# A fused attention and gated-FFN kernel: half batch 1's decay is added by matmuls of its own, and the first values are loaded ahead of its keys

## The chip, the cores and the metric

The kernel runs on one core of one Trainium2 chip. A core has TensorE (matmul), VectorE, ScalarE, GpSimd (POOL in the profile) and SyncE (SP, which here only issues DMAs)[...]. The time is device microseconds; the number to compare is the median of several runs. The profile is of one single execution, with a time and a span of its own.

## The reference

Forgetting attention over 8 batches of 8 heads, 576 positions and 64 elements a head, followed by an FFN with a convolution as a gate:

```python
scores = (1/8) * (q @ k.T)                    # per head, 576 x 576
cum    = cumsum(log(clip(f, 1e-4, 1)))        # per head
scores = where(causal, -1e9, scores + cum[:, None] - cum[None, :])
x      = softmax(scores) @ v                  # heads side by side: 576 x 512
h      = relu(x @ w_in)                       # 576 x 1024
c      = 3-tap convolution of h over the positions, per column
out    = (h * sigmoid(c)) @ w_out             # 576 x 512
```

The difference of the two cum terms is called the decay.

## The kernel before

**Tiling.** The work goes by half batches of four heads (hb, 0 to 15); a pair i is two heads of one of them. For each half batch, q and k are brought in by transposing DMAs that read each float32 as two 16-bit halves (`load_qk`, L110). One tile `stq` of 128 partitions and one tile `stk` hold them, four tiles of each in a ring. Odd partitions hold the high halves, which are bfloat16 numbers; the even ones hold the low halves, which have to be made zero. That is `clamp` (L119), an integer multiply and add on VectorE. The free even partitions carry the decay: partitions 96 and 98 of `stk` get the high and low part of the cumulated logs, with ones opposite in `stq`; partition 126 of `stq` gets the high part, with minus one opposite. So one matmul gives the score with its decay (`scores`, L298).

For half batch 0 these rows come from a quick computation of their own (`rows_first`, L122, issued from ScalarE's and POOL's queues). For half batch 1 and later the clamp covers only partitions 0 to 95 and the others are written by DMA on POOL's queue: the constants by `fill` (L132) from a tile `consts`, which `fill_sources` (L544 to L546) sets on VectorE, and the decay rows by `rows_of`, from SBUF for half batch 1 (L140 to L142) and from a copy `kd` in DRAM for the others (L144, L146). These DMAs wait for the transposes, because they write into the same tile.

**Steps of a pair.** `tail_scores` (L304, once a half batch), `diag_scores` (L330 adds the causal mask by a matmul) and `off_scores` write PSUM; ScalarE takes exponentials (L310, L338, L324); `pv` (L356) multiplies with the values; `norm` (L367, L369) divides on VectorE. Values arrive by plain DMAs in float32 (`load_v`, L163, five instructions for a half batch) in one of two buffers `vf` and are cast on VectorE (L170 to L173). The values of batch b go to buffer b mod 2. A batch's output is transposed on TensorE (L393, L401) and copied out of PSUM (L411, L413).

**FFN.** For each batch eight units of 128 columns: `moe1` (L425, eight matmuls), Relu on ScalarE (L438), two convolution steps on VectorE (L455, L457), tanh on ScalarE (L467), the gate on VectorE (L475). The Relu's output has four buffers `ht`, so the fifth unit's Relu waits for the first unit's gate. `moe2` (L487) multiplies with w_out. The w_in load is released by the first norm (L151, L634). The four w_out loads on POOL's queue (L155) are each released by a one-element memset on VectorE (`hold`, L151).

**Order.** The beginning, to L269, is written out by hand. All after it are tasks, each with engine costs in us, a due time (`key`), dependencies and buffers. At build time `play` walks through an estimated time and gives each engine, when it is free, the ready task with the smallest key. The order that comes out is fixed: on the chip each engine runs its queue in that order, and an instruction whose operand is late holds what is behind it. `lag` is the time that `play` adds for an arrival; SP's loads follow an estimate of the DMA stream (`dma`, `dma_free`, `QUEUED`). After L269 comes first half batch 0 and 1's attention; batch 0's FFN then runs beside half batches 2 and 3, and so on. SP's queue at the start is: q and k of half batch 0 in four pieces (L189, L190), q and k of half batch 1 (L235), the values of both half batches (L251, L252), then the planned loads: q, k, then values of each half batch.

Of the kernel before, what the change touches and what calls it, by code (L numbers as in the profile page):

```python
# [9 lines left out]
FP32 = mybir.dt.float32  # L10
FP16 = mybir.dt.float16
BF16 = mybir.dt.bfloat16
# [6 lines left out]
def kernel(  # L19
# [102 lines left out]
    def rows_first(p, eng):  # L122

        tq, tk, c, r = stq_t[0], stk_t[0], slice(2 * p * S, 2 * (p + 1) * S), slice(64 * p, 64 * (p + 1))
        eng.dma_start(tq[126:127, c], khi4[r, :])
        eng.dma_start(tk[96:97, c], khi4[r, :])
        eng.dma_start(tk[98:99, c], klo4[r, :])
# [7 lines left out]
    def rows_of(hb):  # L135

        tq, tk = stq_t[hb % RING], stk_t[hb % RING]
        c = slice(hb * HH, (hb + 1) * HH)
        if hb == 1:
            nc.gpsimd.dma_start(tk[96:97, 0:HS], khi_sb[c, :])  # L140
            nc.gpsimd.dma_start(tk[98:99, 0:HS], klo_sb[c, :])
            nc.gpsimd.dma_start(tq[126:127, 0:HS], khi_sb[c, :])  # L142
            return
        nc.gpsimd.dma_start(tq[126:127, 0:HS], kd[0:1, c, :].rearrange("j h s -> j (h s)"))  # L144
        row = HS + 64
        nc.gpsimd.dma_start(bass.AP(tensor=tk.tensor, offset=int(tk.offset) + 96 * row, ap=[[2 * row, 2], [1, HS]]),  # L146
                            kd[:, c, :].rearrange("j h s -> j (h s)"))

    def hold(w):

        nc.vector.memset(w[0:1, 0, 0:1], 0.0)  # L151
# [83 lines left out]
    load_qk(1, 0, 4)  # L235
    for side in range(2):
        clamp(0, side, 0, 2)
    rows_first(0, nc.scalar)

# [10 lines left out]
    nc.vector.memset(vf_t[0][0:1, 0, 0, 0:1], 0.0)  # L250
    load_v(0, 0, HH)  # L251
    load_v(0, HH, H)  # L252
# [14 lines left out]
    for t in range(NHT):  # L267
        nc.gpsimd.memset(ht_t[t][:, :, 0:HT_0], 0.0)
        nc.gpsimd.memset(ht_t[t][:, :, HT_0 + S:HT_W], 0.0)  # L269

# [25 lines left out]
    def scores(sc, hb, k0, q0, w, start=True, stop=True):  # L296

        nc.tensor.matmul(sc, stk_t[hb % RING][:, k0:k0 + 128], stq_t[hb % RING][:, q0:q0 + w],  # L298
                         start=start, stop=stop, skip_group_check=True)
# [242 lines left out]
    def fill_sources():  # L542
        z = consts.bitcast(FP32)
        nc.vector.memset(z, 0.0)  # L544
        nc.vector.memset(z[0:2, :], PAIR)
        nc.vector.memset(z[32:33, :], MINUS)  # L546

    CLAMPS, HALVES, LANDING = 8, 16, 3.0
    HELD, POOLED = 4, 4
    WAITS = ((3, 0), (3, 1), (4, 0), (4, 1))  # L550
# [8 lines left out]
    t_fsrc = task({"DVE": 3.1}, [], -9, fill_sources)  # L559
    for hb in range(NHB):  # L560
        key = 2 * hb - 5.5
        ring = [x for j in range(2) for x in t_qk[hb - RING, j]] if hb >= RING else []
        b = hb // 2
        even, landed = [], []
        for s in range(2):
            if hb == 1:
                x = task({"ACT": 0.01}, [], -9, lambda: None, lag=(0.3, 3.8)[s])
            elif hb:
                last = x = task({"SP": 3.0}, ring, key + 0.1 * s, lambda hb=hb, s=s: load_qk(hb, 0, 4, s),
                                lag=LANDING, dma=3.1, behind=last)  # L570
            if hb:
                landed.append(x)
            if hb:
                t = (stq_t, stk_t)[s][hb % RING]
                rows = [(100, 14, 19)] if s else [(96, 15, 0)] + [(0, 48, 33)] * (hb >= CLAMPS)
                even.append(task({"POOL": 0.55 * len(rows)}, [t_fsrc, x], 2 * hb - 3.5,
                                 lambda t=t, rows=rows: [fill(t, *x) for x in rows],
                                 lag=LANDING + 1.0, dma=0.3 if s or hb < CLAMPS else 1.2))
            if hb and (s or hb < CLAMPS):
                even.append(task({"DVE": 0.9}, [x], (2 * hb - 3 if hb > 1 else -5) + 0.2 * s,  # L580
                                 lambda hb=hb, s=s: clamp(hb, s, 0, 4, 96)))
        t_half = None
        if b == 0 and hb < 2:
            t_half = task({"ACT": 0.01}, [], -9, lambda: None, lag=(6.5, 9.3)[hb])
            t_v[b] = t_half
        elif hb < HALVES:
            last = t_half = task({"SP": 3.2}, [t_cast[hb - 4, p] for p in range(2)] if b >= 2 else [], key + 0.2,
                                 lambda b=b, h=HH * (hb % 2): load_v(b, h, h + HH), lag=2.3, dma=3.0, behind=last)
        elif hb % 2 == 0:
            last = t_v[b] = task({"SP": 3.5}, [t_cast[2 * b - j, p] for j in (4, 3) for p in range(2)] if b >= 2 else [],  # L590
                                 key + 1.2, lambda b=b: load_v(b), lag=2.3, dma=6.0, behind=last)
# [4 lines left out]
        if hb:  # L596
            t_rows[hb] = even + [task({"POOL": 1.1 if hb > 1 else 1.6}, landed, 2 * hb - 3.6 if hb > 1 else -9 if hb > 1 else -1.0,
                                      lambda hb=hb: rows_of(hb), lag=LANDING + 1.0)]
        else:
            t_rows[hb] = []  # L600
        for p in range(2):
            t_cast[hb, p] = task({"DVE": 0.75 if p == 0 else 0.42},
                                 [t_half or t_v[b]] + ([t_pv[2 * hb - 5, 1]] if hb >= 3 else []), 2 * hb - 1.1 + 0.5 * p,
                                 lambda hb=hb, p=p: cast_v(hb, p, nc.vector), lag=0.2)

        for p in range(2):
# [10 lines left out]
            x = task({"PE": 0.9}, t_rows[hb], i + 0.1, lambda i=i: diag_scores(i), take="sc")  # L617
            t_qk[hb, p] = [t_tail, x]
            mask = task({"ACT": 1.02}, [x], i + 0.1, lambda i=i: diag_exp(i), take="pm", give=[("sc", x)])
            for s in range(2):  # L620
                x = task({"PE": 0.46}, t_rows[hb], i + 0.2 + 0.4 * s, lambda i=i, s=s: off_scores(i, s),
                         take="sc")
                t_qk[hb, p].append(x)
                exps[s] = task({"ACT": 1.02}, [x] + ([t_pv[i - 2, s]] if i >= 2 else []), i + 0.2 + 0.4 * s,
                               lambda i=i, s=s: off_exp(i, s), give=[("sc", x)])
# [5 lines left out]
            t_norm[i] = task({"DVE": 1.05}, [t_pv[i, 1]], i - 0.0, lambda i=i: norm(i) if i else [norm(i), hold(w_in_f16)],  # L631
                             take="xn" if i % PPB == 0 else None, give=[("O", t_pv[i, 0])])
            if i == 0:
                t_win = task({"POOL": 1.0}, [t_norm[0]], -0.5, lambda: nc.gpsimd.dma_start(  # L634
                    w_in_f16, moe_w_in.rearrange("(cc p) ff -> p cc ff", p=128)), lag=2.0, dma=6.5)
        if hb % 2:
# [10 lines left out]
    start = [PPB * (b0 + nb) + 1.0 for b0, nb in GROUPS]  # L647
    start += [start[-1] + 4.0, start[-1] + 6.0]
    t_exp, t_late = [], []
    for g, (b0, nb) in enumerate(GROUPS):  # L650
# [3 lines left out]
        for ff in range(NFF):  # L654
            key = start[g] + 0.8 * (start[g + 1] - start[g]) * ff / NFF
            relus = []
            for t in range(nt):
# [5 lines left out]
                relus.append(task({"ACT": 0.18 + w / 1200.0}, [x] + relus[0:1], key + 0.05 * t - 1.5,  # L663
# [10 lines left out]
            t_gate[g, ff] = task({"DVE": 0.1 + n / 1800.0 if g == LAST else 0.2 + n / 1050.0}, [x], key - 1.5, lambda g=g, ff=ff: gate(g, ff),  # L674
# [36 lines left out]
    AHEAD, QUEUED = 3.0, 8.0  # L711

    def play():
        busy = {"PE": 11.5, "ACT": 12.0, "DVE": 12.0, "POOL": 14.0, "SP": 19.0}
        ready = {e: [] for e in busy}
        dma_free, clock = 21.5, 0.0
# [112 lines left out]
```

## Time and profile before

| what | us |
| --- | --- |
| median of 7 runs | 272.42 (271.61 to 273.86) |
| profiled execution, its own time | 270.95 |
| its span, first to last instruction | 269.0 |
| TensorE, VectorE, ScalarE busy | 240.9, 226.6, 212.1 |
| first exponential (L338) | 12.22 |
| first score matmul of half batch 1, 2, 3, 4 | 23.88, 41.47, 55.42, 63.96 |
| first FFN matmul (L425) | 36.89 |
| first convolution step (L455) | 39.54 |

The page of the profile gives busy time by engine and, as rows of digits, by 40 slices of 6.7 us each; PEclk is the TensorE clock that was granted, in tenths. Other views give busy time by stretch, the chain of work that ended last (start, duration, what), and the instructions in order of time; there "xN" joins N instructions, and in square brackets is how long the engine was idle before and what it waited for. "SPq", "POOLq" or DMA_DIRECT2D on POOL are issues of DMAs.

### The profile page before, as it was taken

What the parts mean: (1) busy time and instruction counts of PE and PEld (TensorE: products, weight loads), DVE (VectorE), ACT (ScalarE), POOL (GpSimd) and SP (SyncE); (2) the same over time, 40 slices, a digit from 0 to 9 for tenths busy, and PEclk for the clock granted to TensorE, in tenths of its full rate; (3) what the DMA queues carried; (4) which work ended last, traced back from release to release, by engine and by line L of the source; (5) the groups of instructions that cost most, each with busy time, mean ns of one, the idle gap of its engine ahead of it and who ended that gap; (6) DMA issues with size and microseconds to landing.
All of it is one profiled execution on the core that took longest, in us unless ns stands there. A gap on an engine that the chain in (4) does not pass through costs nothing.

```text
span 269.0 us, 6621 instructions
## 1 busy us (share of the span) xinstructions
PE 240.9 (90%) x2602; PEld 165.2 (61%) x2602; DVE 226.6 (84%) x401; ACT 212.1 (79%) x347; POOL 59.4 (22%) x124
## 2 busy tenths in 40 slices
PE   2876769877999999999999999999999999989990
PEld 1344537655767677676777677667776767555640
DVE  5965449999799999999989989999899999978751
ACT  5163639899879999989988999989899998577552
POOL 4481110641222140432404040404110100000000
PEclk9979979999999999999999999999999999999997
DMA  7999999999999999999999999999410202022015
GB/s 143 218 201 198 222 195 227 168 229 178 198 215 196 239 247 168 232 254 264 226 167 226 186 270 162 186 130 257 113 58 23 80 0 77 5 117 80 0 49 225
DMA packets 121284, 44.58 MB, mean 166 GB/s; under 512 B 115560, under 2 KB 116596, under 8 KB 121254
## 3 DMA queue, kind: packets, MB, share of 16 engines
q1 hardware_dynamic: 115088, 32.00, 68.8%
q0 software_dynamic: 5840, 12.01, 17.0%
q8 instruction: 20, 0.33, 0.6%
q10 hardware_dynamic: 326, 0.17, 0.3%
q14 instruction: 10, 0.08, 0.1%
HBM read 13.99 MB, written 9.58 MB: 88 GB/s over the span
## 4 chain that ended last, share of the span: by engine, by line
PE 62%; DMA 9%; DVE 7%; SPq 6%; issue 6%; ACT 6%; POOL 0%; ACTq 0%; DVEq 0%; POOLq 0%
PE mm L425 18%; PE mm L487 18%; PE sc L298 10%; PE O L356 7%; DMA stk<-in_k_dram 6%; SPq L110 4%; PE sc L330 4%; DMA vf<-in_v_dram 2%; PE sc L500 2%; SPq L163 2%; DVE u L457 2%; DVE u L455 2%; PE mm L393 2%; ACT ht L438 1%; DMA out_dram<-ob 1%
## 5 line engine op out<-in xcount | busy, mean ns | idle before, releaser
L425 PE MATMUL mm<-xt,w_in_f 128*128 128x288 f16 x512 | 79.7, 289 | 1.7 <-DVE xt L413 0.4
L298 PE MATMUL sc<-stq,stk 128*128 128x128 bf16 (+3 forms) x576 | 67.4, 243 | 5.6 <-ACT pm L338 3.2
L324 ACT ACTIVATE po<-sc 128x1024 f16<-128x1024 f32 x64 | 64.6, 1028 | 2.1 <-PE sc L298 1.7
L438 ACT ACTIVATE ht<-mm 128x288 f16<-128x288 f32 x128 | 52.0, 414 | 11.5 <-PE mm L425 10.3
L487 PE MATMUL mm<-w_out_f,hg 128*128 128x512 f16 x248 | 58.4, 379 | 0.7 <-ACT xt L411 0.6
L425 PEld LDWEIGHTS <-w_in_f 128*128 128x128 f16 x512 | 47.7, 99 | 18.5 <-issue 3.2
L298 PEld LDWEIGHTS <-stk 128*128 128x128 bf16 x576 | 42.5, 99 | 26.9 <-issue 7.8
L455 DVE SCALAR_TENSOR_TENSOR u<-ht,cwt 128x576 f32<-128x576 f16 x64 | 51.6, 812 | 5.4 <-ACT ht L438 4.7
L457 DVE SCALAR_TENSOR_TENSOR u<-ht,cwt,u 128x576 f32<-128x576 f16 x64 | 51.5, 812 | 0.5
L475 DVE SCALAR_TENSOR_TENSOR hg<-hg,ht 128x576 f16<-128x576 f16 x56 | 41.7, 752 | 3.7 <-ACT hg L467 3.3
L467 ACT ACTIVATE hg<-u,cwt 128x576 f16<-128x576 f32 x56 | 43.4, 780 | 1.0 <-DVE u L457 0.9
L338 ACT ACTIVATE pm<-sc 128x1024 f16<-128x1024 f32 x32 | 32.9, 1027 | 11.8 <-PE sc L298 11.6
L487 PEld LDWEIGHTS <-hg 128*128 128x128 f16 x248 | 23.6, 98 | 24.2 <-issue 0.9
L356 PE MATMUL O<-va,po 128*128 128x65 f16 x640 | 36.5, 194 | 1.2 <-ACT po L324 1.0
L356 PE MATMUL O<-va,pm 128*128 128x65 f16 x256 | 31.1, 194 | 3.0 <-DVE xn L369 1.8
L356 PEld LDWEIGHTS <-po 128*128 128x128 f16 x640 | 30.5, 97 | 2.4 <-ACT po L324 1.8
L132 POOL DMA_DIRECT2D stq<-consts x23 | 12.2, 533 | 73.0 <-PE sc L298 26.2
L356 PEld LDWEIGHTS <-pm 128*128 128x128 f16 x256 | 24.3, 98 | 5.7 <-DVE xn L369 2.7
L369 DVE TENSOR_TENSOR xn<-O,rc 128x640 f16<-128x640 f32 x32 | 26.4, 825 | 1.1
L330 PE MATMUL sc<-trib,identb 128*128 128x512 bf16 x64 | 24.5, 383 | 1.5 <-ACT po L324 1.4
L511 ACT ACTIVATE ob<-mm 128x512 f32<-128x512 f32 x23 | 13.7, 598 | 11.0 <-PE mm L487 10.7
L522 POOL DMA_DIRECT2D out_dram<-ob x10 | 7.5, 748 | 39.9 <-ACT ob L511 20.8
(112 smaller groups left out, 223.2 us busy)
## 6 DMA issues: line engine op xcount, KB each, us to landing
vf<-in_v_dram SPq DMA_DIRECT2D x64, 128.0 KB, 3.9
out_dram<-ob POOLq DMA_DIRECT2D x10, 512.0 KB, 5.1
out_dram<-ob SPq DMA_DIRECT2D x10, 256.0 KB, 2.1
stq<-consts POOLq DMA_DIRECT2D x8, 216.0 KB, 4.5
vf<-in_v_dram SPq DMA_DIRECT2D x16, 64.0 KB, 5.2
w_in_f<-in_moe_w_in_dram POOLq DMA_DIRECT2D x1, 1024.0 KB, 9.1
w_out_f<-in_moe_w_out_dram POOLq DMA_DIRECT2D x4, 256.0 KB, 5.9
out_dram<-ob SPq DMA_DIRECT2D x2, 512.0 KB, 2.8
```

Source lines behind the costliest of these rows:

```text
L298: nc.tensor.matmul(sc, stk_t[hb % RING][:, k0:k0 + 128], stq_t[hb % RING][:, q0:q0 + w], start=start, stop=stop, skip_group_check=True)
L324: nc.scalar.activation(p_of[i, s][:, 0:1024], sc_of.pop((i, s)), AF.Exp, scale=SCALE)
L330: nc.tensor.matmul(sc[:, 512 * s:512 * (s + 1)], identb, trib, start=True, stop=False, skip_group_check=True)
L338: nc.scalar.activation(p_of[i, 2], sc_of.pop((i, 2)), AF.Exp, scale=SCALE)
L356: nc.tensor.matmul(O[:, s, 65 * Q:65 * (Q + 1)], w, va[:, h, m, :], start=(m == 0), stop=(m == Q))
L425: nc.tensor.matmul(ps[:, 0:w], w_in_f16[:, cc, 128 * ff:128 * (ff + 1)], xt[:, cc, w * t:w * (t + 1)], start=(cc == 0), stop=(cc == NCC - 1))
L438: nc.scalar.activation(ht[:, 0, HT_0 + w * t:HT_0 + w * (t + 1)], ps[:, 0:w], AF.Relu)
L455: nc.vector.scalar_tensor_tensor(u, hl, cwt[:, ff, 0:1], hc, op0=ALU.mult, op1=ALU.add)
L457: nc.vector.scalar_tensor_tensor(u, hr, cwt[:, ff, 1:2], u, op0=ALU.mult, op1=ALU.add)
L467: nc.scalar.activation(hv, u, AF.Tanh, scale=cwt[:, ff, 2:3])
L475: nc.vector.scalar_tensor_tensor(hv, hv, 1.0, hc, op0=ALU.add, op1=ALU.mult)
L487: nc.tensor.matmul(ps, chunk(g, ff, c), w_out_f16[:, ff, :], start=(ff == 0), stop=(ff == NFF - 1))
```

## The change

It has four parts.

1. Half batch 1's decay is no longer in `stq` and `stk`. Two new tiles, `dk` and `dq`, lie in the second values buffer, which is free until batch 1's values come. `decay_tiles` sets them on ScalarE: `dk` to zero with minus one in partitions 0 to 2, `dq` to one. `load_decay` writes three rows, on POOL's queue right behind half batch 0's: the high part and the low part into `dk`, the high part into `dq`. Each score matmul of half batch 1 is followed by one of the same shape with these tiles, over all 128 partitions, into the same PSUM. Its clamp covers all 128 partitions, and its two constant fills and three rows are gone. Batch 1's values wait until half batch 1's scores are done.
2. On SP half batch 0's values go ahead of half batch 1's q and k, which are issued later in the program; the values of half batch 1 follow. The memset that held the first values is gone.
3. The constants for half batches 2 and later are set by three tasks on VectorE behind norm(1), no longer at the start. Two w_out loads are released by a later task of half batch 3.
4. Costs, lags and due times of the planner change, with the order that follows from them: norm earlier against clamps and casts, gate later, Relu earlier; half batches 6 and 7 have their q cleared by a DMA fill and no longer by the clamp (`CLAMPS`); from half batch 8 on, values come in whole batches (`HALVES`). Five tasks `warm` of two matmuls each, of which nothing is used, get the lowest priority behind the last pv of half batch 0.

In the resulting order TensorE runs the first pv ahead of off_scores of pair 1; conv_weights after the first off_scores of pair 3; the warm tasks between half batch 1's last pieces; and ten moe1 tiles ahead of half batch 2's scores, where there were six. On VectorE norm(2) and norm(3) are ahead of the clamp of half batch 2's keys, and that clamp comes behind the first convolution step. On ScalarE half batch 2's first exponentials come behind the Relu of the fifth FFN unit and three tanh.

```diff
         c = slice(hb * HH, (hb + 1) * HH)
-        if hb == 1:
-            nc.gpsimd.dma_start(tk[96:97, 0:HS], khi_sb[c, :])
-            nc.gpsimd.dma_start(tk[98:99, 0:HS], klo_sb[c, :])
-            nc.gpsimd.dma_start(tq[126:127, 0:HS], khi_sb[c, :])
-            return
...
+    def decay_tiles(hb, dk, dq):
+        dec_of[hb] = dk, dq
+        for t, x in ((dk, 0.0), (dk[0:3], MINUS), (dq, PAIR)):
+            z = t.bitcast(FP32)
+            nc.scalar.activation(z, one1[0:z.shape[0]].broadcast_to(z.shape), AF.Copy, bias=x, scale=0.0)
+
+    def load_decay(hb):
+        (dk, dq), c = dec_of[hb], slice(HH * hb, HH * (hb + 1))
+        nc.gpsimd.dma_start(dk[0:1, 0:HS], khi_sb[c, :])
+        nc.gpsimd.dma_start(dk[1:2, 0:HS], klo_sb[c, :])
+        nc.gpsimd.dma_start(dq[2:3, 0:HS], khi_sb[c, :])
...
-    load_qk(1, 0, 4)
     for side in range(2):
         clamp(0, side, 0, 2)
     rows_first(0, nc.scalar)
+    load_v(0, 0, HH)
+    load_qk(1, 0, 4)
+    load_v(0, HH, H)
+    early = vf_t[1].rearrange("p h k d -> p (h k d)")
+    decay_tiles(1, early[:, 0:HS // 2 + 32].bitcast(BF16), early[:, HS // 2 + 32:HS + 32].bitcast(BF16))
...
     rows_first(1, nc.gpsimd)
-    nc.vector.memset(vf_t[0][0:1, 0, 0, 0:1], 0.0)
-    load_v(0, 0, HH)
-    load_v(0, HH, H)
+    load_decay(1)
     nc.gpsimd.dma_start(kd[0], khi_sb)
...
+    def warm():
+        ps = mm_pool.tile([128, 512], FP32, name="mm")
+        for t in range(2):
+            nc.tensor.matmul(ps, identb, trib, start=True, stop=True)
...
-                         start=start, stop=stop, skip_group_check=True)
+                         start=start, stop=stop and hb not in dec_of, skip_group_check=True)
+        if hb in dec_of:
+            dk, dq = dec_of[hb]
+            nc.tensor.matmul(sc, dk[:, k0:k0 + 128], dq[:, q0:q0 + w],
+                             start=False, stop=stop, skip_group_check=True)
...
-    CLAMPS, HALVES, LANDING = 8, 16, 3.0
+    CLAMPS, HALVES, LANDING = 6, 8, 3.0
-    WAITS = ((3, 0), (3, 1), (4, 0), (4, 1))
+    WAITS = ((3, 1), (3, 1), (4, 0), (4, 1))
+    WARM = {0: 5}
...
-    t_fsrc = task({"DVE": 3.1}, [], -9, fill_sources)
+    t_dec = {1: task({"ACT": 0.01}, [], -99, lambda: None, lag=4.5)}
     for hb in range(NHB):
+        if hb == 2:
+            t_fsrc = None
+            for z in ((0, 96, 0.0), (0, 2, PAIR), (32, 33, MINUS)):
+                t_fsrc = task({"DVE": 1.03}, [t_norm[1], t_fsrc], 3.0, lambda z=z: fill_source(*z))
...
-            if hb:
+            if hb > 1:
                 t = (stq_t, stk_t)[s][hb % RING]
...
-                even.append(task({"DVE": 0.9}, [x], (2 * hb - 3 if hb > 1 else -5) + 0.2 * s,
-                                 lambda hb=hb, s=s: clamp(hb, s, 0, 4, 96)))
+                even.append(task({"DVE": 0.9}, [x], (2 * hb - 2 if hb > 1 else -5) + 0.2 * s,
+                                 lambda hb=hb, s=s: clamp(hb, s, 0, 4, 96 if hb > 1 else 128)))
...
-            t_norm[i] = task({"DVE": 1.05}, [t_pv[i, 1]], i - 0.0, lambda i=i: norm(i) if i else [norm(i), hold(w_in_f16)],
+            t_norm[i] = task({"DVE": 1.05}, [t_pv[i, 1]], i - 0.5, lambda i=i: norm(i) if i else [norm(i), hold(w_in_f16)],
...
+        if hb in WARM:
+            x = None
+            for _ in range(WARM[hb]):
+                x = task({"PE": 0.44}, [t_pv[2 * hb + 1, 1], x], 999, warm, take="mm", lag=0.05)
+                gives = tasks[x][4]
+                gives.append(("mm", x))
...
-                relus.append(task({"ACT": 0.18 + w / 1200.0}, [x] + relus[0:1], key + 0.05 * t - 1.5,
+                relus.append(task({"ACT": 0.18 + w / 1200.0}, [x] + relus[0:1], key + 0.05 * t - 2.0,
...
-            t_gate[g, ff] = task({"DVE": 0.1 + n / 1800.0 if g == LAST else 0.2 + n / 1050.0}, [x], key - 1.5, lambda g=g, ff=ff: gate(g, ff),
+            t_gate[g, ff] = task({"DVE": 0.1 + n / 1800.0 if g == LAST else 0.2 + n / 1050.0}, [x], key - 0.0, lambda g=g, ff=ff: gate(g, ff),
```

## The prediction

> **What bounds the kernel now.** I read the busy rows by slice first, then busy time by stage, then the chain that ended last over the first 42 us, then the order of instructions there. The page:
>
> ```profile
> span 269.0 us, 6621 instructions
> ...
> PE   2876769877999999999999999999999999989990
> ...
> DVE  5965449999799999999989989999899999978751
> ...
> PEclk9979979999999999999999999999999999999997
> ```
>
> From slice 10 on TensorE is full, and before that it is not. Stages say how much is missing (columns: stretch, length, PE, PEld, DVE, ACT, POOL busy, clock, DMA share, GB/s):
>
> ```profile
> 12.00:19.00 7.00, 4.60 (x34) 2.62 (x32) 4.91 (x8) 4.81 (x6) 6.51 (x27) 0.79 1.05 202
> 19.00:24.00 5.00, 2.85 (x70) 2.48 (x68) 1.54 (x5) 1.39 (x2) 1.68 (x3) 0.96 1.22 187
> 24.00:33.00 9.00, 7.21 (x117) 5.41 (x116) 5.39 (x17) 6.20 (x7) 1.01 (x2) 1.00 1.17 226
> 33.00:37.00 4.00, 1.11 (x18) 0.80 (x15) 2.12 (x4) 0.68 (x1) 1.01 (x2) 0.94 1.26 158
> 37.00:42.00 5.00, 5.00 (x32) 3.18 (x31) 2.35 (x5) 2.72 (x8) 0.50 (x1) 0.71 1.14 240
> 42.00:50.00 8.00, 7.66 (x104) 5.90 (x103) 7.79 (x15) 8.00 (x14) 2.72 (x4) 1.00 1.15 165
> 50.00:60.00 10.00, 7.21 (x83) 5.03 (x81) 9.88 (x22) 8.46 (x16) 4.91 (x7) 1.00 1.28 240
> 60.00:80.00 20.00, 17.99 (x251) 13.49 (x248) 17.86 (x30) 16.99 (x27) 4.52 (x8) 1.00 1.22 196
> 80.00:100.00 20.00, 19.91 (x234) 14.22 (x233) 18.89 (x31) 18.27 (x31) 6.07 (x11) 1.00 1.08 227
> ```
>
> TensorE idles 2.4+2.15+1.8+2.9 us between 12 and 37, 0.3 us to 50, 2.8 us to 60 and 2.0 us to 80; from 80 to 235 all its gaps add to 1.0 us. So the start-up is bound by what arrives when, 42 to 68 by VectorE and ScalarE, the rest by TensorE. A microsecond won before 68 is kept to the end; one won later is not. The chain and the order of work show the start-up's links (start, us, what):
>
> ```profile
> 23.23 10.71 DMA stk<-in_k_dram
> 33.94 0.03 issue
> 33.96 0.88 DVE stk L119
> 34.84 0.14 DVE rc L367
> ...
> 36.89 4.76 PE mm L425 x24
> ```
>
> ```profile
> 19.39 0.50 POOL L142 DMA_DIRECT2D stq<-khi_sb  x1
> ...
> 23.88 0.28 PE L298 MATMUL sc<-stq,stk 128*128 128x64 bf16 x4 [0.98 <-DMA stq<-khi_sb]
> ...
> 42.91 1.02 ACT L338 ACTIVATE pm<-sc 128x1024 f16<-128x1024 f32 x1
> ...
> 47.10 0.73 POOL L155 DMA_DIRECT2D w_out_f<-in_moe_w_out_dram  x1 [5.82 <-DVE w_out_f L151]
> ...
> 55.42 0.27 PE L304 MATMUL sc<-trit,identb 128*128 128x256 bf16 x1
> ```
>
> Half batch 1's scores wait until 23.88 for a decay row issued at 19.39. The normalisation of its last heads (L367, L369) stands on VectorE behind the clamp of half batch 2's keys, which land at 33.94; so the first FFN matmuls start at 36.89. And POOL is held 5.82 us by a w_out load, so half batch 3's decay rows go out only at 47.83 to 49.4 and its scores start at 55.42.
>
> **The change part by part**
>
> *Half batch 1 starts earlier: -2.0 us.* Its three decay rows now go into two ready tiles in the values buffer, straight after half batch 0's rows (POOL, 12.33): issued to 13.9, and at the 4.0 to 4.8 us that these rows took before, landed by 18.7. Its keys go to SP behind five value loads. Those took 3.2 us of SP (12.62 to 15.78), so the keys land at 15.76+3.2 = 19.0 and are clamped by 21.7. What is then last is half batch 0. Its exponentials end at about 21.2, not 20.57, because the first PV matmuls, whose values come early, now stand ahead of the next scores while the clock is at half; the last PV takes 0.45. First scores: 21.9 for 23.88.
>
> The fills of those tiles are three ScalarE instructions of 1152 to 1184 elements; 1024 elements took 1.02, so 3.4 us. ScalarE is free from 8.4, when its row DMAs are out, to the first exponential at 12.22: nothing. If they overran, each microsecond would be one on half batch 0. On POOL the two constant fills and three rows at 17.09 to 19.89 go away and three issues (1.6 us) come in ahead of the kd stores and the memsets; these are needed at 28.6 (kd) and about 17 (the memset that ended at 13.9, now 15.6): nothing. The three constant memsets (3.1 us of VectorE) move to about 23 to 28, where VectorE has gaps (5.39 busy of 9 from 24 to 33): nothing. The w_in load keeps its trigger, norm(0). One wait is new: batch 1's first values, issued by SP at 30.88, overwrite these tiles and so wait for half batch 1's last scores. Behind them on SP are half batch 3's queries and keys. The last scores should end at 21.9+8.9 = 30.8: nothing; each microsecond more delays those keys by one, and they have some 4 us to spare (landed near 45, rows issued at 48.4).
>
> *Its scores cost double: +2.9 us.* 36 added matmuls stream 16x256 + 16x128 + 4x64 = 6400 columns. A 512-column trib matmul is followed by the next after 0.22 us (23.99, 24.21), so they take 2.7 us; each of five warm tasks (two 512-column matmuls) takes 0.43. From first scores to the end of norm(2) the old order took 31.97-23.88 = 8.1 us and was paced by ScalarE. The new one is paced by TensorE: tail 0.33, diagonal twice 1.33, off-diagonal four times 0.87, transpose 0.45, PV twice 0.45, conv weights 0.6, warm twice 0.43 make 9.3. norm(2) no longer hides: conv_weights is behind the third off-diagonal, at +7.55, and its eight small VectorE operations (1.4), the query clamp (0.87) and the norm (1.05) follow it: +10.95.
>
> *norm(3) ahead of the key clamp: -1.35 us.* From norm(2) to the first FFN matmul took 36.89-31.97 = 4.9. Now PV 0.5, warm 0.43, PV 0.45, waits 0.15, norm 1.05 and the old 1.0 for transposes and copies: 3.55. FFN start: 21.9+10.95+3.55 = 36.4, so -0.5.
>
> *The clock: -1.05 us.* The 24 matmuls at 36.89 took 4.76, or 198 ns each; later groups of eight take 0.98, or 122 ns. The granted clock is 0.50 from 36.5 to 39.5. The first convolution came 2.65 after the first matmul; at full clock two groups, two Relus of 0.41 and the hand-over make 1.6. Does the clock hold? It dropped at 16.0 and 36.5, when TensorE had been busy some 1.4 and 0.9 us of the 3.4 before, and held at 22.8 and 26.2 with some 2.2. The Trainium skill, "TensorE: Matmul & The Clock Gate", Part 1 (What's actually happening), gives a free-running window of about 3.4 us and half rate after an idle one. By that rule neither drop had to come, and none could after the change, where no window is idle: -1.05 for certain. By the row a partly busy window drops too. With the new order TensorE is busy about 2.7 us of the last 3.4, or 1.75 if the window falls worse, which is between the drops and the holds; then the term is +0.15. I go by the row and take the clock as held.
>
> *The convolution stretch: +0.3 us.* The first convolution starts at 38.0 for 39.54 (-1.55). From there VectorE is never free. The key clamp (0.80) is now inside it. ScalarE's order has the fourth unit's Relu wait for the first gate, and half batch 2's first exponential stand behind the third tanh: with steps of 0.73 (convolution), 0.68 (gate), 0.80 (clamp), 0.88 (casts) it starts at 47.0 for 42.91. Against that, w_out's loads are behind half batch 3's rows, which go out near 45, so its scores are bound by their turn: about 54.4 for 55.42; and one 1.0 us transpose copy moves from ScalarE to VectorE. Carried through both queues, half batch 4's scores start at about 62.7 for 63.96: -1.25.
>
> *Later parts: -0.5 us.* Relu, gate, cast and norm keys only reorder; two query clamps (0.8 each) become DMA fills. TensorE's gaps were 1.0 us from 80 to 235, so at best that is won; VectorE was idle 1.93 us at 69.4 waiting for norm(8), and the new order puts FFN work there. I take -0.5, bounds -1.0 and +2.0 (an order that starves TensorE). Value loads in whole batches later: DMA has slack by then, nothing. w_out loads a few us later are needed at 75: nothing. In the tail one w_out chunk moves ahead of the last transposes: 0 to +0.9, taken 0.
>
> Sum: -2.0+2.9-1.35-1.05+0.3 = -1.2, -0.5 more: -1.7. On the profiled execution's 270.95 (span 269.0 and 1.95 around it) that is 269.2; the median is 1.47 above it: **270.7 us**.
>
> **The rivals**
>
> *Much is won (0.20).* If TensorE does not pace half batch 1, because pieces overlap that I put end to end, FFN starts near 34.5 and the whole convolution stretch moves with it: -1.9 more, and -0.5 of starvation there: 268.3. For it: VectorE is idle 1.5 us before conv_weights. Against: trib matmuls do follow one another at 0.22.
>
> *No difference (0.25).* The change does not do what it says: rows, keys and values arrive in one stream (DMA share above 1 from 10 us on), and half batch 2's keys at 33.94 and its rows at about 40 stay where they are, so the earlier half batch 1 is eaten by its own 4.8 us of added matmuls. 272.4.
>
> *Slower (0.23).* One mechanism: ScalarE's queue. Relu 4 behind the first gate and the exponential behind the third tanh hold half batch 2 by 4.1 us. That is paid back only if the convolutions start early. It decides at a first convolution of about 39.3: beyond that half batch 4 starts later than 63.96. With a half clock (1.2 later) and half batch 1 at 22.9 the convolution starts at 40.2, half batch 4 at 65, and with +0.4 of reordering the time is 273.9.
>
> **How the numbers follow.** Forecast 0.32 (its own range 269.3 to 271.7), much won 0.20, none 0.25, slower 0.23. About 0.5%, or 1.4 us, is what a measurement of this kernel can tell from no change. Below 271.06 lie most of the forecast and all of the much-won case: 0.50; above 273.8, most of the slower case and a little of none: 0.22; 0.28 between. The range reaches into both ends and leaves 0.1 out at each: 267.3 to 274.4.
>
> **What would show it.** Right: first scores of half batch 1 near 21.9, FFN near 36.4 at clock 1.0, first convolution near 38, half batch 2's first exponential near 47, half batch 3's scores near 54.4, half batch 4's before 63, TensorE's gaps from 80 to 235 at about 1. Wrong: the decay rows waited for (later than 21.9), clock 0.5 after 36, a VectorE wait for half batch 1's values, SP held at batch 1's values because the decay tiles in that buffer are still read after 30.9, or new gaps on TensorE after 80.

## The result and the profile after

The changed kernel is slower: 276.91 us median of 12 runs (274.04 to 281.56), against 272.72 of 31 runs of the kernel before on the same chip. The ratio is 1.0121, 95% interval 1.0094 to 1.0148. The ratios in this document are taken over undisturbed executions alone and the medians over all of them, so the two need not agree (the two medians alone would give 1.0154). The profiled execution took 274.42 us, its span is 272.2. The forecast was 270.7.

The page of the profile of the changed kernel, the rows shown of the kernel before:

```profile
span 272.2 us, 6675 instructions
...
PE   2657979599999999899999999999999999989991
...
DVE  5714657969999999699899899999899899988651
...
PEclk9979999979999999999999999999999999999997
```

In the third slice, 13.6 to 20.4 us, TensorE's digit is 5 for 7 and VectorE's 1 for 6. The busy times by stretch put it more closely (columns as in the prediction):

```profile
12.00:19.00 7.00, 2.25 (x13) 1.48 (x14) 1.84 (x4) 4.20 (x4) 3.96 (x8) 0.84 1.13 220
...
33.00:37.00 4.00, 2.60 (x36) 1.78 (x34) 2.98 (x11) 2.31 (x3) 0.43 (x1) 1.00 0.33 70
37.00:42.00 5.00, 4.44 (x56) 3.01 (x57) 1.34 (x3) 1.35 (x2) 0.00 (x0) 1.00 0.96 188
42.00:50.00 8.00, 6.51 (x54) 4.38 (x53) 7.32 (x12) 5.26 (x13) 2.71 (x4) 1.00 1.28 190
50.00:60.00 10.00, 7.89 (x97) 6.07 (x95) 8.02 (x17) 8.03 (x12) 2.68 (x3) 0.83 1.02 186
60.00:80.00 20.00, 19.06 (x258) 13.97 (x255) 19.54 (x35) 19.18 (x30) 6.31 (x11) 1.00 1.14 207
```

TensorE did 4.60 us of work from 12 to 19 before and does 2.25 now. From 60 on it is fuller than before (19.06 of 20 for 17.99), so the loss is not there. ScalarE's instructions in that stretch, in order of time, in the kernel before and then in the changed one ("ACTq" is the issue of a DMA):

```profile
6.54 0.51 ACTq L125 DMA_DIRECT2D stq<-khi  x1
7.27 0.48 ACTq L126 DMA_DIRECT2D stk<-khi  x1
7.79 0.61 ACTq L127 DMA_DIRECT2D stk<-klo  x1
```

```profile
8.56 0.57 ACTq L125 DMA_DIRECT2D stq<-khi  x1
10.77 0.49 ACTq L126 DMA_DIRECT2D stk<-khi  x1
12.52 0.47 ACTq L127 DMA_DIRECT2D stk<-klo  x1
13.04 3.46 ACT L152 ACTIVATE vf<-one 128x1184 f32<-128x1184 f32 x3 [6.74 <-DMA stk<-khi]
18.23 1.02 ACT L361 ACTIVATE pm<-sc 128x1024 f16<-128x1024 f32 x1 [1.73 <-PE sc L317]
```

The three decay rows of half batch 0, which the diff does not touch, go out 2.0, 3.5 and 4.7 us later. The fills of half batch 1's decay tiles stand behind them, and the first exponential comes at 18.23 for 12.22. The chain that ended last says what the third row waited for (start, duration, what):

```profile
8.78 0.51 SPq L174
9.33 3.17 DMA vf<-in_v_dram
12.52 4.14 DMA stk<-klo
...
16.75 0.58 PE sc L317 x4
```

The third row is issued at 12.52, as the fourth load of batch 0's values (L174), issued at 9.33, has landed. The two share no data. What they share is a semaphore: a semaphore is a counter that tells an engine that something is done. In the built program SP's and ScalarE's DMAs take eight of them in turn for their completion, and ahead of a DMA stands a wait until the DMA eight earlier, which last used its semaphore, has landed. For the three rows the program has these waits; DMAHW0 to DMAHW7 are the eight semaphores:

```
row (line)  before                     after
L125        DMAHW1: queries, heads 0-1 DMAHW5: queries of heads 2 and 3
L126        DMAHW2: fsb                DMAHW7: first value load
L127        DMAHW4: cwrow              DMAHW2: fourth value load
```

`fsb` holds f and `cwrow` the weights of the convolution; the loads of both are issued by 1.45 us in the kernel before. So there these waits cost nothing.

From there everything is 4.2 to 5.4 us behind the forecast. Half batch 1's first score is at 26.09 (forecast 21.9), the first FFN matmul at 40.72 (36.4), the first convolution at 42.68 (38.0), half batch 4's first score at 68.09 (62.7).

### The profile page after: what moved, and what is told of

Same layout as the page of the kernel before. It is cut to its first block, busy times and chain, and to the rows that moved or that the text cites. A ratio compares the mean times of both kernels' runs of the same rounds, so it can differ in the third digit from the quotient of the medians.

```text
span 272.2 us, 6675 instructions
## 1 busy us (share of the span) xinstructions
PE 245.3 (90%) x2648; PEld 168.8 (62%) x2648; DVE 224.4 (82%) x400; ACT 214.4 (79%) x348; POOL 59.9 (22%) x124
## 4 chain that ended last, share of the span: by engine, by line
PE 68%; DVE 10%; DMA 8%; ACT 5%; SPq 4%; issue 2%; DVEq 0%; ACTq 0%
PE mm L448 18%; PE mm L510 18%; PE sc L317 12%; PE O L379 9%; DMA vf<-in_v_dram 7%; PE sc L353 4%; SPq L110 2%; DVE u L480 2%; PE sc L523 2%; SPq L174 2%; PE mm L416 2%; DVE xn L392 2%; DVE hg L498 2%; DMA stk<-klo 2%; DVE u L478 1%
## 5 line engine op out<-in xcount | busy, mean ns | idle before, releaser
L317 PE MATMUL sc<-stq,stk 128*128 128x128 bf16 (+3 forms) x576 | 70.3, 244 | 8.7 <-DMA stk<-klo 5.3
L317 PEld LDWEIGHTS <-stk 128*128 128x128 bf16 x576 | 43.7, 99 | 29.6 <-issue 12.8
L379 PE MATMUL O<-va,po 128*128 128x65 f16 x640 | 37.3, 195 | 0.1
L379 PEld LDWEIGHTS <-po 128*128 128x128 f16 x640 | 31.1, 99 | 1.3 <-ACT po L347 0.4
L379 PEld LDWEIGHTS <-pm 128*128 128x128 f16 x256 | 24.7, 99 | 6.2 <-DVE xn L392 3.6
L132 POOL DMA_DIRECT2D stq<-consts x24 | 12.7, 532 | 70.9 <-DMA stq<-in_q_dram 35.0
L534 ACT ACTIVATE ob<-mm 128x512 f32<-128x512 f32 x24 | 14.3, 597 | 11.3 <-PE mm L510 11.0
L390 DVE RECIPROCAL rc<-O 128x10 f32<-128x10 f32 x32 | 6.9, 217 | 13.6 <-PE O L379 13.4
```

What stands on the lines that cost most here:

```text
L379: nc.tensor.matmul(O[:, s, 65 * Q:65 * (Q + 1)], w, va[:, h, m, :], start=(m == 0), stop=(m == Q))
```

## The experiments

The first four share one series of the kernel before (median 272.39, 29 runs). Theory 1 is the shared semaphores, theory 2 the traffic of the value loads, theory 3 the doubled score matmuls and the new order of the convolution stretch.

### Half batch 0's rows on GpSimd's queue

```diff
-    rows_first(0, nc.scalar)
+    rows_first(0, nc.gpsimd)
```

> The changed kernel with one word different: half batch 0's three decay rows are issued from GpSimd's queue instead of ScalarE's. Theory 1 (the rows' DMAs stand behind the landing of the DMA eight earlier among SP's and ScalarE's, which in the changed kernel is a load of values): the rows go out by 8.3, the first scores come at 11.5 to 12.5 instead of 16.75, half batch 1's first scores at about 22.2, the FFN at about 37 (T0 + 14.6), half batch 4's scores at about 63.5, and the time is about 271 (270 to 272.4), some 4 us under the changed kernel. Theory 2 (the value loads ahead delay the rows' own transfer): issued early, the rows still land at 14 or later, the time stays above 274. Theory 3 (the doubled score matmuls and the new plan of the convolution stretch cost the time, whoever issues the rows): first scores at 12, and yet half batch 4's scores at 66 or later and the time above 274.

269.58 us, a little under the expected range; ratio to the kernel before 0.9914 (0.9886 to 0.9943). In the built program GpSimd's DMAs use other semaphores; the value loads still go out from 7.25 on. GpSimd's issues, in order of time, and TensorE's first scores and first FFN matmuls:

```profile
6.75 0.70 POOL L125 DMA_DIRECT2D stq<-khi  x1 [2.80 <-DVE stq L119]
7.59 0.54 POOL L126 DMA_DIRECT2D stk<-khi  x1
8.12 0.52 POOL L127 DMA_DIRECT2D stk<-klo  x1
...
12.09 0.38 PE L317 MATMUL sc<-stq,stk 128*128 128x128 bf16 x4 [0.52 <-DMA stk<-klo]
...
35.51 0.41 PE L448 MATMUL mm<-xt,w_in_f 128*128 128x288 f16 x2 [0.38 <-DVE xt L436]
```

One word makes a kernel that is 1.2% slower into one that is 0.9% faster, with the doubled matmuls, the new order and the early value loads all in it. Theories 2 and 3 fall as the cause of the loss.

### The same move in the kernel before

> The kernel before with half batch 0's three decay rows issued from GpSimd's queue: the control for the first run of this group. All theories: rows out at 6.6 to 8.3 as before, first scores at 11.4 to 12.3, the time within 0.6 us of the kernel before (272.4), so that what the first run gains over the kernel before is the change's own.

273.63, ratio 1.0051 (1.0023 to 1.0079): 1.2 us, twice the bound that all theories gave. The rows go out at 7.21 to 8.52 and the first scores are at 13.18 for 11.36. So the move costs the kernel before something, and what it gains in the changed kernel is not a merit of GpSimd's queue.

### The changed kernel with the old order of loads

```diff
-    load_v(0, 0, HH)
     load_qk(1, 0, 4)
+    load_v(0, 0, HH)
     load_v(0, HH, H)
```

> The changed kernel with the order of the loads on SP as it was before: half batch 1's queries and keys ahead of batch 0's values. Now no value load is ahead of the rows in the traffic, but the DMA eight before each row in the order of the build is the first keys', half batch 1's queries' and the second value load's. Theory 1: the third row is held until that second value load, issued at about 13.5, has landed: it goes out at about 16 to 17, later than in the changed kernel (12.52), first scores at about 20, and the time is 2 to 5 us above the changed kernel's. Theory 2: rows out at about 6.5 to 7.8 as before, first scores at 11.4 to 12, time 271 to 272.5. Theory 3: as the changed kernel within 1 us.

280.35 of four executions, ratio 1.0320 (1.0269 to 1.0372). ScalarE's issues in order of time:

```profile
6.51 0.52 ACTq L125 DMA_DIRECT2D stq<-khi  x1
12.21 0.51 ACTq L126 DMA_DIRECT2D stk<-khi  x1
16.74 0.47 ACTq L127 DMA_DIRECT2D stk<-klo  x1
```

With no value load ahead of them the rows are later still, because the count of DMAs gives them the semaphores of `cwrow`, of half batch 1's queries and of the second value load. (The expectation had the first keys in place of `cwrow`; the built program has `cwrow`, loaded long before, and the first row does go out without delay, at 6.51.) This is the sharpest test of theory 1: traffic would have let the rows out early. The kernel before has the same order of loads and on-time rows: there a memset ahead of the value loads put them behind the rows in the count.

### The kernel before with the early value loads alone

```diff
-    load_qk(1, 0, 4)
     ...
     rows_first(0, nc.scalar)
+    load_v(0, 0, HH)
+    load_qk(1, 0, 4)
-    nc.vector.memset(vf_t[0][0:1, 0, 0, 0:1], 0.0)
-    load_v(0, 0, HH)
     load_v(0, HH, H)
```

> The kernel before with one move: batch 0's first value loads go ahead of half batch 1's queries and keys on SP. No decay matmul, no tiles in the values buffer, the plan of before. Theory 1: the rows go out at 8.6, 10.8 and 12.5 as in the changed kernel, first scores at about 16.7, half batch 1's at 27 to 28, and the time is 275.5 to 277, 3 to 4.5 us slower than before. Theory 2: rows out at 6.5 to 7.8, landing some 2 us later: 273 to 274.5. Theory 3: 272 to 273, about as before.

The rows do what theory 1 says, and the time does not: 273.41, ratio 1.0031 (0.9991 to 1.0071), for an expected 3 to 4.5 us. In order of time:

```profile
8.38 0.55 ACTq L125 DMA_DIRECT2D stq<-khi  x1
10.63 0.48 ACTq L126 DMA_DIRECT2D stk<-khi  x1
12.45 0.47 ACTq L127 DMA_DIRECT2D stk<-klo  x1
...
16.68 0.58 PE L297 MATMUL sc<-stq,stk 128*128 128x128 bf16 x4 [5.36 <-DMA stk<-klo]
...
27.22 0.72 PE L297 MATMUL sc<-stq,stk 128*128 128x64 bf16 x8
```

The first scores are 5.3 us late, half batch 1's 3.3 (27.22 for 23.88), the first FFN matmul 1.8 (38.68 for 36.89), the first convolution 1.1 (40.63 for 39.54), half batch 4's scores 0.8 (64.75 for 63.96). At half batch 1's scores, the FFN and half batch 3 the kernel before waited for something that does not move with half batch 0, as the prediction's own first section lists: a decay row, half batch 2's keys, w_out. By this reading these waits took the delay up; no run takes a single one of them out. Between the FFN and the convolution it was the clock: the 24 first FFN matmuls ran at clock 1.00 and took 3.69 us, where the kernel before had 0.50 and 4.76, and the convolution came 1.95 behind the first of them for 2.65. The change moves these waits, so in the changed kernel the lateness goes through whole: against the run with the rows on GpSimd's queue the first scores are 4.7 us late, half batch 1's 5.2, the FFN 5.2, the convolution 5.2, the span 5.2 (272.2 for 267.0). Against a second profiled execution of that kernel (see the filler matmuls below) half batch 1, the FFN and the convolution are each 3.4 or 3.5 late and the span 3.6.

### Early values, rows in time, decay rows added as before

The edits of the last run and of the first together, on the kernel before.

> The kernel before with two edits: batch 0's first values ahead of half batch 1's keys on SP (as in the run b_v_early), and half batch 0's rows from GpSimd's queue (as in b_rows_pool). It prices the early values alone, rows in time, decay rows added as before. If the gain of the run a_rows_pool is the early values' alone: half batch 1's first scores at 22 to 23, time 269.5 to 271. If it needs the added decay matmuls too (half batch 1's rows behind the constant fills hold its scores in the order of before): first scores at 23.5 to 26, time 272.5 to 274, as b_rows_pool (273.6) or 1 us under it.

274.52 for 272.09 in its series, ratio 1.0080 (1.0050 to 1.0110), half a microsecond above the expected range. TensorE's first scores of half batch 1:

```profile
26.95 0.37 PE L297 MATMUL sc<-stq,stk 128*128 128x64 bf16 x4 [3.88 <-DMA stq<-khi_sb]
```

They wait 3.88 us for a decay row that went out at 20.20. (The profiled execution took 278.59, 4.1 us above the median, so the size of the wait may not be the usual one.) The ratio is no better than that of the rows on GpSimd's queue alone, 1.0051: so the early values alone gain nothing. The other half was tried too, with the rows on ScalarE:

### Rows on ScalarE and in time, with and without early values

```diff
     rows_first(0, nc.scalar)
+    nc.scalar.copy(vf_t[0][0:1, 0, 0, 0:1], one1[0:1])
     load_v(0, 0, HH)
```

> The changed kernel with one instruction more: a one-element copy on ScalarE behind the three decay rows writes into the first element of the values buffer, so that the first value loads are issued behind the rows, by SP at about 8.5 for 7.6, and come behind them in the build's count of DMAs too. The rows stay on ScalarE's queue; the order and the sizes of SP's loads stay as they are. Theory 1 (a row waits for the landing of the DMA eight earlier): the DMAs eight ahead of the rows are now the first loads of the program, long landed, so the rows go out at 6.5, 7.3 and 7.8 as before the change, first scores at 11.4 to 11.8, half batch 1's at 20.2 to 21, time 268.3 to 270.3, no slower than the run with the rows on GpSimd's queue (269.6). Theory 2 (the traffic of the values): most of it still runs beside the rows, so they land at 13 or later: 272 or more.

The rows are issued at 6.72 to 7.99, the first scores come at 12.03 without a wait, half batch 1's at 21.1: theory 1 again. But the time misses the expected 268.3 to 270.3: the six executions lay between 268.1 and 280.9 (median 274.12), too far apart for a ratio. What happens is in the trace, issues by SP and GpSimd and VectorE's work in order of time:

```profile
19.88 9.19 SPq L110 DMA_TRANSPOSE stq<-in_q_dram  x1
20.30 0.98 POOL L663 DMA_DIRECT2D w_in_f<-in_moe_w_in_dram  x1 [1.92 <-DVE w_in_f L162]
32.65 0.88 DVE L119 TENSOR_SCALAR stq<-stq,lim 96x2304 uint16<-96x2304 uint16 x1 [2.47 <-DMA stq<-in_q_dram]
33.44 0.21 DVE L391 RECIPROCAL rc<-O 128x10 f32<-128x10 f32 x1
```

The transposing load of half batch 2's queries lands 12.7 us after its issue, with w_in's 1 MB beside it; its clamp waits, and norm(2) stands behind the clamp: 33.44 for 30.66 in the run with the rows on GpSimd's queue. FFN at 39.66.

The same kernel with half batch 1's queries and keys ahead of the values:

> As the run a_hold, but half batch 1's queries and keys go ahead of batch 0's values on SP, as they did before the change. It prices the moved loads alone, with the rows on time. If the early values are what starts half batch 1 early (the first step of the prediction): first scores at 11.4 to 11.8, half batch 0's first division at about 20.3 for 18, half batch 1's first scores at 22 to 22.7, and the time 1.2 to 2 us above a_hold's. If the values are not what sets it (the keys or the decay rows are): within 0.5 us of a_hold's.

273.42, ratio 0.9999 (0.9968 to 1.0031); half batch 1 starts at 23.57, the first division is at 21.36 for 18.91, FFN at 38.20. Beside a_hold's own noise no difference of times can be given, but against the rows-on-GpSimd run (20.89, 35.51) half batch 1 and the FFN are 2.7 us later and the gain over the kernel before is gone. Against that kernel's second profiled execution (22.64, 37.27) they are 0.9 later. With the last run: no kernel without both the early values and the added decay matmuls shows a gain. Whether the two are enough is not shown, as the new order and the moved constants are in every kernel that gains.

With the decay tiles in a buffer of their own:

> As the run a_hold, with the two tiles of half batch 1's decay in a buffer of their own instead of in batch 1's values buffer. Batch 1's values are then loaded without waiting for half batch 1's last scores. If that wait was hidden, as the prediction had it: SP's value loads at about 24 instead of 30, and the time within 0.4 us of a_hold's. If SP's queue held at the values cost something downstream (half batch 3's queries and keys behind them): 0.5 to 1.5 us below a_hold's.

268.8 to 282.2 in six executions, median 276.17. The queries met w_in's load here too (issues at 19.88 and 19.71, 8.72 us), and SP reached batch 1's values only at 32.94. So this run says nothing of the wait that it was to price.

### w_in's load moved away from the queries

A first edit moved only the mark (a one-element write that holds the load back) behind the second division. The load then went out ahead of its mark, at 18.3 to 18.8, and VectorE's mark waited for it to land, 6.2 us with the rows on ScalarE and 10.9 with them on GpSimd:

> As the run a_hold, with the load of w_in (1 MB, on GpSimd's queue) released by the second division instead of by the first: it goes out at about 22.5 for 20.3, 2.6 us behind the issue of half batch 2's queries instead of 0.4. Theory 4 (in a_hold the transposing load of half batch 2's queries met w_in's load, took 12.7 us instead of 9, and norm(2) stood behind its clamp on VectorE): the queries' issue takes about 3.6 us for 9.2, their clamp waits for nothing, norm(2) at about 30.5 for 33.4, the FFN at about 35.3 for 39.7, and the time is 267.5 to 269.5, steadily. If the long issue of the queries is not w_in's doing: it stays at 9 us and the time at 272 to 275.

276.35 for 271.73, ratio 1.0119 (1.0065 to 1.0174); with the rows on GpSimd's queue 278.27, 1.0183. These runs do not test what they were to test, since the load was early and not late. Mark and load moved together, on top of the one-element copy of the kernel above (the load's own task then issues nothing):

```diff
-    norm(i) if i else [norm(i), hold(w_in_f16)]
+    norm(i) if i != 1 else [norm(i), hold(w_in_f16), load_w_in()]
```

> As the run a_hold, with both the mark that releases w_in's load and the load itself moved behind the second division (in the run a_hold_w1 only the mark had moved: the load went out ahead of it, at 18.4, and VectorE's mark then waited 6.2 us for it to land). w_in's load goes out at about 22.5, 2.6 us behind half batch 2's queries. Theory 4 (w_in's load beside the transposing load of half batch 2's queries makes that load slow, and norm(2) stands behind the queries' clamp): queries' issue 3.6 us for 9.2, clamp and norm(2) at about 30 for 32.7 and 33.4, FFN at about 35.3 for 39.7, time 267.5 to 269.5. If the long load of the queries is not w_in's doing: issue still 9 us, time 272 to 275.

```profile
21.03 2.75 SPq L110 DMA_TRANSPOSE stq<-in_q_dram  x1
...
22.77 0.79 POOL L166 DMA_DIRECT2D w_in_f<-in_moe_w_in_dram  x1 [4.22 <-DVE w_in_f L162]
...
30.34 0.87 DVE L119 TENSOR_SCALAR stq<-stq,lim 96x2304 uint16<-96x2304 uint16 x1
```

The queries' issue is short, the clamp waits for nothing, and the FFN starts at 35.98, 3.7 us earlier than without the move (expected 35.3). The time is not as expected: 273.13, as in the kernel before that ran beside it, ratio 0.9989 (0.9965 to 1.0012). Now the keys' load meets w_in (issue 8.77 us), SP issues its loads from 35 to 62 some 1.7 to 4.8 us behind the rows-on-GpSimd run, and the values of half batch 3 are cast at 62.17 for 58.10; the chain that ended last leads there through the loads of these values. So it looks as if SP's queue took back what half batch 1 won; no run tests this by itself.

With the rows on GpSimd's queue:

> As the run a_rows_pool (half batch 0's rows on GpSimd's queue), with w_in's load and its mark behind the second division, at about 22. Theory 4: the queries' load is as in a_rows_pool or shorter, time 268.5 to 269.8. If w_in's load is now late for the first FFN matmul or meets the keys' load: 270.5 or more.

271.91, ratio 0.9940 (0.9916 to 0.9964), no better than without the move.

### The filler matmuls

```diff
-    nc.tensor.matmul(ps, identb, trib, start=True, stop=True)
+    nc.tensor.matmul(ps[:, 0:16], identb, trib[:, 0:16], start=True, stop=True)
```

The kernel of the first run was measured again beside it:

> The kernel of the run a_rows_pool once more, as the measure for the next run and as a second look at its gain. If the gain over the kernel before is the kernel's own: ratio to before 0.989 to 0.995, FFN at about 35.5. If it was that chip's: above 0.997.

270.77, ratio 0.9942 (0.9917 to 0.9967). The gain is there again, but the FFN starts at 37.27, not at about 35.5. The same kernel thus has two profiled executions, and they differ in the granted clock, in the third and the eighth slice:

```profile
PEclk9999999998899999999999999999999999999999
```

```profile
PEclk9979999799999999999999999999999999999998
```

In the second, from 17 to 20 us, the clock is 0.50 for 1.00, half batch 1 starts at 22.64 for 20.89, and the span is 268.6 for 267.0. A difference of 1.7 us at one place between single profiles is therefore within what this kernel does by itself.

> As a_rows_again, with the ten filler matmuls of half batch 1 cut from 512 to 16 columns, the order of all instructions kept. If the fillers hold the clock (the prediction's fourth step, about 1 us): granted clock near 0.5 between 24 and 40, first convolution about 1 us later than 37.5, time 0.7 to 1.5 us above a_rows_again's. If the clock is lost but the microsecond is taken up later, where VectorE, ScalarE and SP set the pace: convolution later, time within 0.5 us. If the fillers do nothing: clock and convolution as in a_rows_again.

269.59, ratio 0.9899 (0.9869 to 0.9930). In the profiled execution the clock does fall, by stretch:

```profile
36.00:38.00 2.00, 0.23 (x5) 0.11 (x4) 0.29 (x1) 1.01 (x1) 0.00 (x1) 0.73 1.15 249
38.00:40.00 2.00, 1.85 (x8) 1.19 (x9) 0.00 (x0) 0.41 (x1) 0.00 (x0) 0.50 1.79 202
```

and the first convolution comes at 40.81 for 39.23, 1.6 us late. But the clock is only part of it, for the first FFN matmuls wait for w_in's load:

```profile
38.15 7.46 PE L448 MATMUL mm<-xt,w_in_f 128*128 128x288 f16 x36 [1.92 <-DMA w_in_f<-in_moe_w_in_dram]
```

They start 0.9 us later (38.15 for 37.27), and from there to the convolution it is 2.66 for 1.96, so 0.7 is the clock's; and the clock falls while TensorE waits. That execution was 3.0 us above the kernel's median, so it is not the typical one. With w_in's load moved, rows on ScalarE, nothing waits for w_in in either profile; there too the clock is 0.50 from 35 to 41 without the fillers and 1.00 with them, and the way from FFN to convolution is 2.64 for 1.96.

The time without the fillers is no longer; the two intervals overlap a little, with the better ratio on the side without them. On the kernel with w_in's load moved the pair gave 0.9989 with fillers and 0.9975 (0.9949 to 1.0000) without; on the one with only its mark moved 1.0119 and 1.0135 (1.0074 to 1.0196). The kernel with the rows on ScalarE and in time gave 0.9982 (0.9957 to 1.0006) without them, at 273.04, and has no ratio with them. In these profiles the fillers hold the clock, and they buy no time that these runs can see; where the lost 0.7 us is made up is open.

## Why the prediction was wrong

The step that failed is the first, "Half batch 1 starts earlier: -2.0 us", and in it one sentence: "ScalarE is free from 8.4, when its row DMAs are out, to the first exponential at 12.22: nothing." It took the rows' issue times from the trace of before, though the change puts value loads ahead of them in the count. What happened in its place: the third row went out at 12.52 for 7.79, and half batch 1 started at 26.09. With the rows in time the kernel took 269.58 and 270.77 in its two series, about the forecast's 270.7; but its terms are off there by about a microsecond either way and in part cancel, so some of that agreement is luck (start times in us; "again" is the second profiled execution; the forecast's span is its 269.2 less the 1.95 around it):

| | forecast | changed kernel | rows on GpSimd | again |
| --- | --- | --- | --- | --- |
| half batch 1, first scores | 21.9 | 26.09 | 20.89 | 22.64 |
| from there to the end of norm(2) | 10.95 | 10.84 | 10.84 | 10.84 |
| first FFN matmul | 36.4 | 40.72 | 35.51 | 37.27 |
| first convolution | 38.0 | 42.68 | 37.47 | 39.23 |
| half batch 2, first exponential | 47.0 | 51.64 | 46.43 | 48.19 |
| half batch 3, scores | 54.4 | 60.08 | 53.45 | 56.64 |
| half batch 4, scores | 62.7 | 68.09 | 61.46 | 65.24 |
| from there to the end | 204.5 | 204.1 | 205.5 | 203.4 |
| span | 267.2 | 272.2 | 267.0 | 268.6 |

- *Half batch 1 starts earlier.* Forecast -2.0, measured +2.2: 4.2 of the 5.0 us by which the span misses. The rule left out is the wait for the DMA eight earlier. The prediction's price for the fills, "if they overran, each microsecond would be one on half batch 0", names the place and looks at the wrong overrun. With the rows in time the start lies on both sides of the forecast, which had the half clock in it: 20.89 without it, 22.64 with it.
- *Its scores cost double.* 10.84 for 10.95: right.
- *norm(3) ahead of the key clamp.* From norm(2) to the FFN 3.79 (40.72 less 36.93) for 3.55: right within 0.24.
- *The clock.* It was held from 33 to 50 in the changed kernel, and the 36 first FFN matmuls took 5.50, 153 ns each. The time to the first convolution fell from 2.65 to 1.96, so 0.7 of the 1.05. As a gain in the end it is not shown, as the filler runs say. The Trainium skill, "TensorE: Matmul & The Clock Gate", Part 1 (What's actually happening), has the clock drop after an idle window; the rows side with the prediction's reading that a partly busy one is enough. In the changed kernel:

```profile
48.00:50.00 2.00, 0.85 (x11) 0.57 (x9) 2.00 (x4) 1.35 (x3) 0.00 (x0) 1.00 1.91 76
50.00:52.00 2.00, 1.01 (x9) 0.68 (x7) 2.00 (x4) 1.04 (x2) 0.00 (x0) 1.00 0.68 96
52.00:54.00 2.00, 0.99 (x9) 0.59 (x9) 2.00 (x6) 2.00 (x3) 0.57 (x1) 1.00 1.19 243
54.00:56.00 2.00, 2.00 (x27) 1.66 (x25) 1.46 (x4) 1.92 (x4) 2.00 (x3) 0.58 1.12 235
```

  TensorE was busy 2.85 us of these six, with no gap longer than 1.7, and then had half its clock, which by an idle window alone was not due.
- *The convolution stretch.* From the first convolution to half batch 4's scores 25.4 for 24.7; with the rows on GpSimd's queue 24.0 and 26.0. ScalarE's in-order wait for the gates is there (TensorE waits 1.15 and 1.68 us for exponentials at 49.4 and 52.7), at the forecast size: 8.96 from the convolution to half batch 2's first exponential, in all three profiles, for 9.0. Not in the forecast is a second half clock behind these waits. The changed kernel has it from 54 to 58, the execution "again" from 51 to 54, the first one on GpSimd's queue not at all; from the exponential to half batch 3's scores they took 8.44, 8.45 and 7.02.
- *Later parts.* Forecast -0.5 on the 205.0 of before, with bounds of -1.0 and +2.0; -0.9, +0.5 and -1.6 in the three, the last outside the bounds.
- *Batch 1's values on SP.* Forecast at 30.88 for nothing; in the changed kernel SP reached them with the keys' issue done at 24.9 and sent them at 35.23, when half batch 1's last scores were through. The DMA share of 0.33 from 33 to 37 is that hole. Half batch 3's rows still went out at 44.37 and 45.64, well ahead of its scores at 60.08. So nothing shows that the wait cost time there; the run that was to price it, with the decay tiles in a buffer of their own, does not say.

Of the rivals, "slower" had the direction, and its sign came out: a first convolution past 39.3 makes half batch 4 late (42.68, 68.09). It was too small, 1.5 us for 3.3 by the ratio, and its trigger, a half clock at the first FFN matmuls, did not occur: what it had right, it had by luck. "No difference" had one stream of rows, keys and values as its reason; with the rows in time the change does make a difference, and in the changed kernel the third row's 4.14 us from issue to landing, against 3.57 before (7.79 to the first scores at 11.36), puts the traffic at some 0.6 us for that row.

## What to carry to other kernels

When a change puts DMAs ahead of others, list for each later DMA which one is eight before it in the build, on all queues that share the semaphores, and take its landing as a wait, data or not. Late work costs what the waits behind it do not take up: a change that removes such waits also makes every other delay, here one of its own making, count in full. And a gain at the front has to be followed through the queue of loads, which moves with it and meets other transfers.

## What the hardware showed that was not expected

The transposing load of half batch 2's queries and w_in's load meet or miss by a microsecond, in the one profile that there is of each kernel. Where w_in's load was issued from 2.1 us before to 0.4 us after the queries (five kernels), the queries' issue on SP took 8.3 to 9.2 us; where it came 0.6 to 3.8 us after (eleven profiles), 2.6 to 4.3. In nine of the latter the keys' load, issued next, took 7.6 to 10.2 us in its place, in two 3.5 and 4.5. How often single executions fall to one side or the other, and so how much of the spread of these kernels it makes, is open.

The fastest kernels by ratio are the changed kernel with half batch 0's rows on GpSimd's queue, 0.9914 and 0.9942 of the time before, and the same with the fillers cut, 0.9899.
